# Issuing V of the later batches from GpSimd instead of SyncE in a fused attention and MLP kernel

## The chip, the cores and the metric

The kernel runs on one core of one Trainium2 chip. The metric is the device time of one execution in microseconds. Three runs of the kernel before gave 335.32, 333.19 and 333.25 us, with the median at 333.25 us. One more execution was recorded by the hardware profiler; all views of the profile come from that one.

Engines are called as in the profile: PE is TensorE (its weight loads are PEld), DVE is VectorE, ACT is ScalarE, POOL is GpSimd, SP is SyncE. SP computes nothing here and only issues DMAs; SPq in the profile is its instruction queue.

## The reference

Two stages follow each other. The first is a block-causal attention over 8 batches and 8 heads with 576 positions of 64 elements: a position sees all keys of its own block of 64 and of the blocks before it. The second is an MLP without bias, from 512 to 2048 and back, with a swish of slope beta per hidden unit.

```python
scores = scale * np.matmul(q, k.transpose(0, 1, 3, 2))          # [8, 8, 576, 576]
scores = np.where(block_i >= block_j, scores, -1000000000.0)     # blocks of 64
attn = np.exp(scores - max); attn = attn / (sum(attn) + 1e-09)
x = matmul(attn, v)                                              # -> [4608, 512]
h = x @ w_in                                                     # [4608, 2048]
g = h * (1.0 / (1.0 + np.exp(-beta * h)))
return (g @ w_out).astype(np.float32)                            # [4608, 512]
```

All inputs and the output are float32 in memory; the kernel computes on bf16 and f16 copies.

## The kernel before

**Tiling.** The attention goes in 32 units, four pairs of heads in each of the eight batches b. For a unit, PE multiplies K with Q (L708), ACT takes the exponential (L724), PE multiplies the result with V and with a column of ones for the sum (L764, 30 small matmuls), and DVE divides (L776, L783). The MLP goes in nine chunks of 512 rows. A chunk has 16 groups of four matmuls with w_in (L1000), a tanh on ACT (L1010), a product on DVE (L1014), and then the product with w_out: the plain form for the first chunk (L1036) and a scheme with seven products of half size for the others (L921, with its sums and differences on DVE, L885).

**How Q and K come.** For the first two batches they are loaded in small pieces (L618), cast on POOL (L625) and turned on PE (L634). From b = 2 on (QB is 2), a load brings Q or K of four heads in f32 (L654), POOL casts it to bf16 in two halves (L665), and one DMA transpose turns Q and K of these four heads together (L672); this is called the crossbar's turn here. There are twelve, two per batch. From b = 3 on (XB is 3), the attention's result is turned in the same way by DMA (L800). All these loads and turns are issued by SP, one after the other.

**How V comes.** V of one batch is 1.18 MB in f32. It is loaded by six DMAs: four with 128 positions of all heads (L548, 128 partitions of 8 x 64 elements, 256 KB) and two that bring the last 64 positions, for the even and for the odd heads (L551, 64 KB each). They go into a staging buffer Vs in f32. POOL then casts it, four times two heads, into Vn in bf16 (L574), and L764 reads Vn. The list PARTS says, for each batch, which heads are loaded by whom. In b = 0, four heads of the last pieces are loaded by POOL, cast on the way, straight into Vn; all others are loaded by SP into Vs. Vs has two slots: one of its own and one in the second half of OV. From b = 2 on only the first is used (ts.only), since OV then holds operands of the MLP. So V of a batch may be loaded only after POOL has cast the batch before.

**What sets the order.** A planner (class Plan) lays out all operations at build time. Each operation has an engine, a cost in ns, a priority (lower goes first), dependences and tiles; the planner takes, whenever an engine is free in its own clock, the ready operation of the lowest priority. The order it finds is written out as fixed instruction streams, one per engine, with semaphore waits. On the chip each engine works strictly in that order. For DMAs the planner keeps two queues, H for those that SP and ACT issue and S for those that POOL issues, with a transfer time for each (xfer, 1400 ns for a full piece of V) and a rule for their sharing.

The cost of a V issue is given as 300 + 550 n ns on SP, and 150 + 1450 n ns on POOL, with n = 1 for a full piece and 0.25 for a small one. The loads of SP are also put in one sequence by hand (seq): Q and K of a batch, then its V, each after the one before.

```python
for b in range(B):
    for u in range(4 * b, 4 * b + 4):
        ...
        if u == 4 * b + (3 if b < 2 else 1):
            seq += [o for h0, _, e, _ in PARTS[b] if e == "SP" for o in ld["V", b, h0]]
for x, y in zip(seq, seq[1:]):
    y.after = x
```

POOL's own stream, from about 40 us on, consists of the last weight loads (L507), V's casts (L574) and the casts of Q and K (L665). The weights' DMAs and those few of V in b = 0 are all that POOL's queue (q0) carries; SP's is q1, and the stores of ACT and SP are in the profile's lists of issues under their own lines.

Of the kernel before, what the change touches and what calls it, by code (L numbers as in the profile page):

```python
# [359 lines left out]
def bass_blockwise_causal_attn__then__act_swish_beta_kernel(  # L360
# [10 lines left out]
    with es:  # L371
        def sb(name, shape, dt):
            return es.enter_context(nc.sbuf_tensor(name, shape, dt))
# [1 line left out]
        NQ = 2  # L375
        QB, XB, CAST = 2, 3, "POOL"
        NE = 3
        PARTS = [((0, 4, "SP", range(6)), (4, 8, "SP", range(2)), (4, 8, "POOL", range(2, 6)))] + [((0, 8, "SP", range(6)),)] * 7
        GROUPS = [((0,), (1,), (2,), (3,))] + [((0, 1), (2, 3))] * 7
        NS = 6  # L380
        JOIN = (2,3,4,5,6,7)
# [8 lines left out]
        Vs = [sb("Vs0", [128, 5, 8, 64], f32), OV[:, 2560:5120].rearrange("p (t h d) -> p t h d", t=5, h=8)]  # L390
# [4 lines left out]
        Vn = [sb(f"Vn{i}", [128, 5, 8, 66], bf16) for i in range(NQ)]  # L395
# [25 lines left out]
        P = Plan()  # L421
# [6 lines left out]
        def mm(n):  # L428
            return max(n / 2.4 + 3, 55.0)
# [8 lines left out]
        def pr(u):  # L438
            b, c = divmod(u, NPAIR)
            return u if b < 1 else 10 * u if b < 2 else 994 + 100 * (b - LAG) + 4.9 * c  # L440
# [14 lines left out]
        def mk(fn):  # L455
            return lambda g, e: fn(g)
# [13 lines left out]
        for i in range(NQ):  # L470
# [5 lines left out]
            o = P.op("POOL", 200, mk(lambda g, i=i: g.memset(Vn[i][:, 4, :, 64:66], 0.0)), prio=-5)  # L476
# [6 lines left out]
        for i in range(NQ, NE + 1):  # L483
# [4 lines left out]
                  xfer=100, dma=("d_beta", 1), prio=0.1)  # L488
# [28 lines left out]
        for i in range(NFILL):  # L517
# [10 lines left out]
            n = 125  # L528
            o = P.op("PE", n, ff, deps=[c2, c4], tiles=[tf], lat=n, mode="full", prio=1e6 + i)
# [4 lines left out]
        load, ld, early = {}, {}, []  # L534
        tl = {}
        for b in range(B):
            ts, t = P.tile("Vs"), P.tile("V")
            ts.only = (b,) if b < 2 else (0,)
            early += [ts] * (b < 2)
            tl[b] = t  # L540
            for h0, h1, e, tt in PARTS[b]:

                vs = []
                for i in tt:
                    def fv(g, e, ts=ts, t=t, b=b, h0=h0, h1=h1, i=i):
                        d = Vn[t.slot] if e == "POOL" else Vs[ts.slot]
                        if i < 4:
                            return [g.dma_start(d[:, i, h0:h1, 0:64],  # L548
                                                v[b, h0:h1, 128 * i:128 * i + 128, :].rearrange("h p d -> p h d"))]
                        o = i - 4  # L550
                        return [g.dma_start(d[64 * o:64 * o + 64, 4, h0 + o:h1:2, 0:64],  # L551
                                            v[b, h0 + o:h1:2, 512:576, :].rearrange("h p d -> p h d"))]

                    n = (h1 - h0) / 8 * (1 if i < 4 else 0.25)
                    if e == "SP":
                        o = P.op("SP", 300 + 550 * n, fv, tiles=[ts], xfer=1400 * n,
                                 prio=3.5 + 0.1 * (h0 > 0) if b == 0 else 4 * b + (3.5 if b < 2 else 0.5),
                                 dma=["d_V", h0, 1])
                    else:
                        o = P.op("POOL", 150 + 1450 * n, fv, tiles=[t], xfer=1400 * n, prio=-30 if b == 0 else 4 * b + (3.5 if b < 2 else 0.5), dma=["d_VP", h0, 1])  # L560
                        o.after = lastv if b else None
                    vs.append(o)
                ld["V" if e == "SP" else "VP", b, h0] = vs
                if e == "POOL":
                    lastv = vs[-1]
                    for h in range(h0, h1, 2):
                        load.setdefault(4 * b + h // 2, []).extend([*vs, *ones, *vzero])
                    continue
                n = 5 if 4 in tt else len(tt)
                for g0 in range(h0, h1, 2):  # L570
                    g1 = g0 + 2

                    def fw(g, e, ts=ts, t=t, g0=g0, g1=g1, n=n):
                        return g.tensor_copy(Vn[t.slot][:, 0:n, g0:g1, 0:64], Vs[ts.slot][:, 0:n, g0:g1, :])  # L574

                    o = P.op("POOL", 60 + 60 * n * (g1 - g0), fw, deps=[*vs, *ones, *vzero], tiles=[ts, t],
                             prio=4 * b + 0.5 - (38.5 - 4.6 * (h0 > 0)) * (b < 1))
                    for h in range(g0, g1, 2):
                        load[4 * b + h // 2] = [o]
                lastv = o  # L580
# [12 lines left out]
        def blocks(b):  # L593
            x0 = S * b % RX
            n = min(5, (RX - x0) // 128)
            return [z for z in ((0, n, x0), (n, 5 - n, 0)) if z[1]]
# [4 lines left out]
        for u in range(NU):  # L601
            b, c = divmod(u, NPAIR)
# [7 lines left out]
            if b < QB:  # L610

                turned = []
                for w, (nm, src) in enumerate((("Q", q), ("K", k))):
                    ts, pt = P.tile("ST"), P.tile("P1")
# [6 lines left out]
                    o = ld[nm, u] = P.op("SP", 420, fl, tiles=[ts], xfer=1170, prio=u, dma=["d_S", 0, 1])  # L621
                    o.pkt = 80.0

                    def fn(g, e, ts=ts, tn=tn, p=p, w=w):
# [4 lines left out]
                    o = P.op("POOL" if onp else "DVE", 850 if onp else 750, fn, deps=[o], tiles=[ts, tn],  # L629
                             prio=-40 + 3 * u if onp else -1)  # L630

                    def ft(g, e, tn=tn, pt=pt, p=p, w=w):
                        for i in range(6):
# [4 lines left out]
                    o = P.op("PE", 6 * 43, ft, deps=[o, c4], tiles=[tn, pt, tt_], lat=6 * 43 + 170, mode="full",  # L638
                             prio=pr(u))
# [8 lines left out]
            elif p == 0:  # L648

                for w, (nm, src) in enumerate((("Q", q), ("K", k))):  # L650
                    ts = P.tile("S4")

                    def fl(g, e, ts=ts, src=src, b=b, c=c):
# [3 lines left out]
                    o = P.op("SP", QKI, fl, deps=[o for t in early6 for o in t.users] if b == QB else [],  # L657
                             tiles=[ts], xfer=QKX, prio=u, dma=["d_S4", 0, 1])
# [20 lines left out]
            if b not in JOIN or p == 0:  # L679
# [4 lines left out]
                for grp in visits:  # L684
# [3 lines left out]
                    def fq(g, e, pst=pst, grp=grp, tqk=tqk, b=b):  # L688
                        keep = {}
                        for (uu, g0), ps in zip(grp, pst):  # L690
# [4 lines left out]
                            for t, q0, q1, off in blocks:  # L695
# [17 lines left out]
                    n = sum(220 if g0 < 3 else 60 for _, g0 in grp)  # L713
                    o = P.op("PE", n, fq, deps=cps, tiles=list({id(x): x for x in pst}.values()) + [tqk] + [tes[uu] for uu in sorted({uu for uu, _ in grp})] * (b > 0),
                             lat=n + 200, mode="row", prio=pr(u) + .2 if len(grp) == 4 else pr(u + 1) + .1 if grp[0][0] > u else
                             pr(u) + .1 + .1 * (grp[0][1] >= 2))
# [3 lines left out]
            for g0 in range(4):  # L720
                o, ps = qk[g0]
# [76 lines left out]
            if b >= XB:  # L798
                def fy(g, e, tx=tx, c=c, b=b):
# [4 lines left out]
                n = len(blocks(b))  # L804
                xt.append(P.op("SP", 1300 * n, fy, deps=nrm + (xt[u - 4:u - 3] if b > XB else []), tiles=[tx], xfer=1100,
                               prio=-1, dma=[f"d_TX{n}_", 0, n]))
# [32 lines left out]
        for b in range(B):  # L839
            for u in range(4 * b, 4 * b + 4):  # L840
# [3 lines left out]
# [3 lines that stand above are left out]
# [142 lines left out]
        for r in range(NRC):  # L989
# [5 lines left out]
            for j in range(NJ):  # L995
                ph, tt = P.tile("P1"), P.tile("th")

                def fh(g, e, ph=ph, j=j, row=row):
                    for c in range(4):
# [4 lines left out]
                o = P.op("PE", 4 * mm(512), fh, deps=xd + [win[j // 4]], tiles=[ph, tg], lat=4 * mm(512) + 170,  # L1004
                         mode="full", prio=1000 + 100 * r + j)
# [21 lines left out]
            for w, d0, d1 in [(w, 0, DM) for w in range(4)]:  # L1027
# [4 lines left out]
                o = None  # L1032
                for j0, j1 in parts:
                    def fo(g, e, po=po, tg=tg, w=w, j0=j0, j1=j1, d0=d0, d1=d1):
                        for j in range(j0, j1):
# [4 lines left out]
                    n = (j1 - j0) * mm(d1 - d0)  # L1040
                    was = o
                    o = P.op("PE", n, fo, deps=gs[j0:j1] + wout[j0 // 4:(j1 + 3) // 4],
                             tiles=[po, tg], lat=n + 170, mode="full",
                             prio=1000 + 100 * r + (16 + w + 0.01 * j0 if w == 0 else
                                                     103 + 5.33 * (w - 1) + 1.33 * j0 / 4))
# [84 lines left out]
```

## Time and profile before

| | before |
|---|---|
| median of three runs | 333.25 us |
| profiled execution, device time | 333.59 us |
| its span | 331.8 us |
| instructions | 7478 |
| granted PE clock, mean | 1.0 |
| DMA packets, bytes | 154,993, 53.41 MB |
| of them under 512 B | 139,072 |
| V into Vs from SP, full pieces | 24, median 4.2 us to landing |
| L574 on POOL | 28 casts from Vs, 21.0 us busy, 94.6 us idle ahead of them |
| L665 on POOL | 48 casts, 38.1 us busy, 27.6 us idle ahead |
| L672 from SP | 12 turns, median 7.4 us to landing |
| L800 from SP | 24 turns, median 3.7 us to landing |

The span is the time from the first to the last instruction in the trace; the device time of the same execution is 1.8 us longer. The profiled execution took 0.34 us more than the median of the runs.

A row of a time line gives the start and the length in us, the engine, the line with operation and operands, and the count; brackets at its end give the idle time before it and what ended that. Rows of SPq are issues: their length is the time in which SP was held, not the transfer. A row of windows gives its bounds, its length, then the busy time of PE, PEld, DVE, ACT and POOL, with counts, the PE clock, the share of the DMA engines (the sum over queues, so that it can exceed 1) and GB/s. The table of queues has packets, MB and the share that their packets took of 16 engines' span. In the views of waits, a row has the waiting engine and line, the releaser, the total in us, the number of waits and the longest.

### The profile page before, as it was taken

To read this page: it belongs to the slowest core of one execution; us is meant where nothing else is said; L and a number is where in the kernel's file an instruction comes from. 1 tells how busy PE (TensorE), PEld (TensorE's weight loads), DVE (VectorE), ACT (ScalarE), POOL (GpSimd) and SP (SyncE) were. 2 spreads that over 40 slices of the span, in tenths; PEclk is the share of its full clock that TensorE was granted. 3 is DMA by queue.
4 is the path that set the end of the run, shared out by engine and by line. 5 is a ranking of instruction groups with operands and counts; after the bars stand their busy time and mean duration, and the time that the engine had idled before them with its cause. 6 is when DMAs were issued, how large, how long until landed. Compare 5 with 4: busy or idle time off the path is not lost.

```text
span 331.8 us, 7478 instructions
## 1 busy us (share of the span) xinstructions
PE 321.0 (97%) x3112; PEld 204.1 (62%) x3090; DVE 222.0 (67%) x448; ACT 212.6 (64%) x324; POOL 85.4 (26%) x127
## 2 busy tenths in 40 slices
PE   7898999999999999999999999999999999999996
PEld 4575455545586557754665666576566766666685
DVE  4637775679763898358966595678467685666742
ACT  2876974298457886768757856874875555544521
POOL 6757181056073053103630730240000000000000
PEclk9999999999999999999999999999999999999999
DMA  8999999999999999999999998989102310110023
GB/s 194 227 223 241 207 206 197 210 277 226 189 272 210 210 233 181 201 201 202 179 196 219 221 240 187 158 144 157 35 34 40 87 50 34 55 42 32 2 96 126
DMA packets 154993, 53.41 MB, mean 161 GB/s; under 512 B 139072, under 2 KB 154448, under 8 KB 154960
## 3 DMA queue, kind: packets, MB, share of 16 engines
q1 hardware_dynamic: 141200, 40.19, 64.3%
q0 software_dynamic: 5568, 4.36, 8.4%
q10 hardware_dynamic: 8192, 8.39, 8.1%
q8 instruction: 24, 0.39, 0.5%
q14 instruction: 9, 0.07, 0.1%
HBM read 36.71 MB, written 9.44 MB: 139 GB/s over the span
## 4 chain that ended last, share of the span: by engine, by line
PE 86%; ACT 3%; DVE 2%; SPq 2%; DMA 2%; issue 2%; POOL 1%; POOLq 0%
PE PS L1000 36%; PE PS L921 29%; PE PS L764 8%; PE PS L708 7%; PE PS L1036 4%; DMA Vs<-in_v_dram 2%; ACT E L724 2%; SPq L548 2%; PE PS L813 1%; DVE gT L1014 1%; ACT th L1010 1%; ACT xq L788 1%; DVE xq L783 0%; SPq L551 0%; PE PS L634 0%
## 5 line engine op out<-in xcount | busy, mean ns | idle before, releaser
L1010 ACT ACTIVATE th<-PS,beta 128x512 f32<-128x512 f32 x144 | 96.4, 699 | 59.9 <-PE PS L1000 58.4
L1000 PE MATMUL PS<-xT,w_in 128*128 128x512 bf16 x542 | 130.0, 379 | 2.9 <-issue 0.6
L1014 DVE SCALAR_TENSOR_TENSOR gT<-th,PS 128x512 f16<-128x512 f32 x144 | 95.2, 682 | 30.9 <-ACT th L1010 30.2
L724 ACT ACTIVATE E<-PS 128x1024 bf16<-128x1024 f32 x93 | 92.1, 1028 | 28.4 <-PE PS L708 28.4
L1000 PEld LDWEIGHTS PS<-xT,w_in 128*128 128x128 bf16 x576 | 53.4, 98 | 55.6 <-DVE gT L1014 2.0
L921 PE MATMUL PS<-w_out,gT 128*128 128x256 f16 x512 | 63.0, 273 | 0.0
L921 PEld LDWEIGHTS PS<-w_out,gT 128*128 128x128 f16 x512 | 49.0, 98 | 12.1 <-issue 1.7
L574 POOL CAST Vn<-Vs 128x640 bf16<-128x640 f32 (+1 forms) x28 | 21.0, 751 | 94.6 <-DMA Vs<-in_v_dram 93.2
L665 POOL CAST QKn<-ST 128x640 bf16<-128x640 f32 x48 | 38.1, 794 | 27.6 <-DMA ST<-in_q_dram 13.6
L708 PE MATMUL PS<-QKT 64*128 64x320 bf16 (+4 forms) x328 | 36.4, 297 | 0.2 <-ACT E L724 0.2
L764 PEld LDWEIGHTS PS<-Vn,E 128*128 128x128 bf16 x930 | 30.9, 97 | 4.2 <-POOL Vn L574 0.6
L942 ACT ACTIVATE ost<-PS 128x512 f32<-128x512 f32 x32 | 19.4, 606 | 21.5 <-PE PS L921 21.5
L764 PE MATMUL PS<-Vn,E 128*128 128x65 bf16 x930 | 31.9, 193 | 0.4 <-POOL Vn L574 0.4
L921 PE MATMUL PS<-OV 128*128 128x256 f16 x256 | 32.0, 273 | 0.0
L708 PEld LDWEIGHTS PS<-QKT 64*128 64x128 bf16 (+1 forms) x328 | 13.4, 96 | 25.7 <-issue 11.2
L921 PEld LDWEIGHTS PS<-OV 128*128 128x128 f16 x256 | 24.2, 98 | 5.8 <-issue 0.8
L783 DVE TENSOR_TENSOR xq<-PS,inv 128x640 bf16<-128x640 f32 x30 | 24.7, 822 | 0.8
L885 DVE TENSOR_TENSOR OV<-gT 128x1024 f16<-128x1024 f16 x32 | 24.3, 767 | 1.1 <-PE PS L921 0.6
L730 DVE MEMSET E<- 64x64 uint32 x62 | 6.9, 112 | 23.8 <-ACT E L724 21.8
L945 DVE SCALAR_TENSOR_TENSOR ost<-PS,ost 128x512 f32<-128x512 f32 x22 | 15.1, 688 | 8.3 <-PE PS L921 5.9
L921 PE MATMUL PS<-OV,gT 128*128 128x256 f16 x128 | 16.1, 273 | 0.0
L1036 PE MATMUL PS<-w_out,gT 128*128 128x512 f16 x64 | 15.5, 380 | 0.0
(65 smaller groups left out, 176.1 us busy)
## 6 DMA issues: line engine op xcount, KB each, us to landing
out_dram<-ost ACTq DMA_DIRECT2D x32, 256.0 KB, 4.2
ST<-in_q_dram SPq DMA_DIRECT2D x12, 576.0 KB, 5.7
ST<-in_k_dram SPq DMA_DIRECT2D x12, 576.0 KB, 7.4
Vs<-in_v_dram SPq DMA_DIRECT2D x24, 256.0 KB, 4.2
ST<-in_q_dram SPq DMA_DIRECT2D x8, 288.0 KB, 5.7
ST<-in_k_dram SPq DMA_DIRECT2D x8, 288.0 KB, 6.4
w_in<-in_moe_w_in_dram POOLq DMA_DIRECT2D x4, 512.0 KB, 10.7
w_out<-in_moe_w_out_dram POOLq DMA_DIRECT2D x4, 512.0 KB, 10.1
```

What stands on the lines that cost most here:

```text
L574: return g.tensor_copy(Vn[t.slot][:, 0:n, g0:g1, 0:64], Vs[ts.slot][:, 0:n, g0:g1, :])
L665: return g.tensor_copy(QKn[tn.slot][:].rearrange("p a w n -> p (a w n)")[:, 640 * (2 * a + w):][:, 0:640] .rearrange("p (t h d) -> p t h d ...
L708: z = g.matmul(o, QKT[tqk.slot][r, uu % 2, 1, 128 * t + y:128 * t + m + y], x)
L724: return g.activation(E3[es_(te)][:, g0, :, :], PS[:, ps.slot:ps.slot + 2, :], ACT.Exp, scale=0.125)
L764: z = g.matmul(o, eblk(te, t, i, h), Vn[Tv.slot][:, t, 2 * c + h, 0:65], start=(t == 0), stop=(t == i))
L783: return g.tensor_tensor(xq[xq_(tx)][:].rearrange("p i (h d) -> p h i d", h=2), both(pv, 0, 64), x, ALU.mult)
L885: return P.op("DVE", dve_t(SZ * HC / 2), mk(lambda g: g.tensor_tensor(fo(), fx(), fy(), op)), deps=deps, tiles=tiles, prio=prio)
L921: x = g.matmul(PS[:, pw.slot, HM * w:HM * w + HM], fa()[:, j, 128 * w:128 * w + 128], fb()[:, j, :], start=first and (pair or w == 0) and ...
L1000: z = g.matmul(PS[:, ph.slot, :], w_in[:, c, 128 * j:128 * j + 128], xT[:, c, row % RX:row % RX + RC], start=(c == 0), stop=(c == 3))
L1010: return g.activation(th[tt.slot][:], PS[:, ph.slot, :], ACT.Tanh, scale=beta[:, j:j + 1])
L1014: return g.scalar_tensor_tensor(out=gT[tg.slot][:, j, :], in0=th[tt.slot][:], scalar=1.0, in1=PS[:, ph.slot, :], op0=ALU.add, op1=ALU.mult)
L1036: z = g.matmul(PS[:, po.slot, 0:d1 - d0], gT[tg.slot][:, j, 128 * w:128 * w + 128], w_out[:, j, d0:d1], start=(j == 0), stop=(j == NJ - 1))
```

## The change

From b = 2 on, the six DMAs of V are issued by POOL (a new kind of part, "POOLF") rather than by SP. They bring the same f32 rows to the same staging buffer Vs, and the casts L574 stay. The cost that the planner is told is that of a POOL issue, the priority is 4 b + 0.5, as it was on SP, and a batch's first issue comes after the last cast of the batch before (lastv), the others one after the other. As only parts of SP go into the sequence made by hand, V of these batches leaves it. V of b = 0 and b = 1 is loaded as before. The planner then lays out all five engines anew.

```diff
-        PARTS = [((0, 4, "SP", range(6)), (4, 8, "SP", range(2)), (4, 8, "POOL", range(2, 6)))] + [((0, 8, "SP", range(6)),)] * 7
+        PARTS = [((0, 4, "SP", range(6)), (4, 8, "SP", range(2)), (4, 8, "POOL", range(2, 6)))] + [((0, 8, "POOLF" if b in range(2, 8) else "SP", range(6)),) for b in range(1, 8)]
...
-                        d = Vn[t.slot] if e == "POOL" else Vs[ts.slot]
+                        d = Vn[t.slot] if e == "POOL" and b < 1 else Vs[ts.slot]
...
+                    elif e == "POOLF":
+                        o = P.op("POOL", 150 + 1450 * n, fv, tiles=[ts], xfer=1400 * n, prio=4 * b + 0.5, dma=["d_VF", h0, 1])
+                        o.after = vs[-1] if vs else lastv
                     else:
                         o = P.op("POOL", 150 + 1450 * n, fv, tiles=[t], xfer=1400 * n, prio=-30 if b == 0 else 4 * b + (3.5 if b < 2 else 0.5), dma=["d_VP", h0, 1])
                         o.after = lastv if b else None
                     vs.append(o)
-                ld["V" if e == "SP" else "VP", b, h0] = vs
+                ld["VP" if e == "POOL" else "V", b, h0] = vs
```

## The prediction

> **What bounds the kernel now.** I read the busy shares and the chain of waits first, then the busy time by windows, then the waits by engine, and last the time lines of SP, GpSimd (POOL) and TensorE (PE) around the third and fourth batch (b = 2 and 3).
>
> ```profile
> PE 321.0 (97%) x3112; PEld 204.1 (62%) x3090; DVE 222.0 (67%) x448; ACT 212.6 (64%) x324; POOL 85.4 (26%) x127
> ...
> PE 86%; ACT 3%; DVE 2%; SPq 2%; DMA 2%; issue 2%; POOL 1%; POOLq 0%
> ```
> PE is busy for 321.0 of 331.8 us, and 86% of the chain runs through it. So 10.8 us are idle in all. The windows (length, then PE busy time) say where:
> ```profile
> 0.00:20.00 20.00, 16.77 (x197) 11.04 (x199) 10.27 (x29) 12.10 (x17) 11.65 (x32) 1.00 1.03 199
> 20.00:40.00 20.00, 18.07 (x258) 10.81 (x253) 14.49 (x33) 14.87 (x31) 11.05 (x15) 1.00 1.10 239
> 60.00:80.00 20.00, 19.79 (x109) 8.65 (x105) 15.43 (x28) 14.61 (x22) 8.03 (x10) 1.00 1.17 243
> 220.00:240.00 20.00, 19.74 (x183) 12.47 (x179) 14.40 (x28) 13.84 (x21) 1.44 (x2) 1.00 0.51 91
> ```
> 5.2 us of the gap (3.23 + 1.93) lie ahead of 40 us. From 40 to 320 us the fourteen windows leave 2.8 us together, and some 2.8 us are the end (last eviction and store). The DMA share (last column but one) is above 1.0, queues overlapping, until 220 us and falls to 0.51 then: the transfers are nearly full, but hidden behind PE.
>
> The V transfers are waited for, but by an engine off the path:
> ```profile
> POOL Vn L574 <- DMA Vs<-in_v_dram: 93.2, 7, 18.9
> ```
> No such wait of PE after 40 us is over 0.2 us, except where the trace names none. What counts is the slack between V or Q/K and the PE instruction that needs them:
> ```profile
> 42.76 12.61 SPq L548 DMA_DIRECT2D Vs<-in_v_dram  x3
> 55.41 8.05 SPq L672 DMA_TRANSPOSE QKT<-QKn  x1
> 98.52 3.61 SPq L548 DMA_DIRECT2D Vs<-in_v_dram  x1
> 102.23 3.91 SPq L672 DMA_TRANSPOSE QKT<-QKn  x1
> ```
> ```profile
> 69.03 3.56 POOL L574 CAST Vn<-Vs 128x640 bf16<-128x640 f32 x4 [15.68 <-DMA Vs<-in_v_dram]
> 92.47 3.41 POOL L574 CAST Vn<-Vs 128x640 bf16<-128x640 f32 x4 [10.04 <-DMA Vs<-in_v_dram]
> 95.94 3.48 POOL L665 CAST QKn<-ST 128x640 bf16<-128x640 f32 x4
> ```
> ```profile
> 80.81 1.97 PE L764 MATMUL PS<-Vn,E 128*128 128x65 bf16 x60
> 114.44 0.39 PE L708 MATMUL PS<-QKT 64*128 64x512 bf16 x2
> ```
> For b = 2, V lands at 69.0, its first cast ends near 69.9, and the first L764 that reads it runs at 80.8: 11 us of slack. For b = 3 the cast at 92.5 stands ahead of the Q/K casts at 95.9 on POOL, these ahead of the crossbar's turn at 102.2 on SP; with the median 7.4 us to landing (the page's issue table) it is there at 109.6, and its first L708 runs at 114.4: 4.8 us. Counted the same way, later V casts lead their first L764 by 12 us or more (154.2 against 170.2, and wider).
>
> [...] between 42 and 62 us, with weights on q0, both queues made progress (2112 and 7902 packets). [...] no V issue of the size wanted here is in the trace.
>
> **The change part by part.**
> ```profile
> q1 hardware_dynamic: 141200, 40.19, 64.3%
> q0 software_dynamic: 5568, 4.36, 8.4%
> L548 POOL DMA_DIRECT2D Vn<-in_v_dram x2: 740/745/750, 11.4 to 12.1; - x2
> L551 POOL DMA_DIRECT2D Vn<-in_v_dram x2: 614/616/619, 12.8 to 14.2; - x2
> DMA to landing us min/median/max: 8.0/10.1/14.1
> ```
> *Off SP:* 36 issues, four of 1024 rows of 256 B and two of 256 rows for each of six batches. Their rows after 42 us on SP's time line add up to 46.0 us[...]. None of it is on PE's path, so the credit there is zero. What goes is order: Q/K loads no longer stand behind V, nor V behind SP's wait for an xq (L800).
>
> *On POOL:* 512 rows cost 745 ns and 128 rows 616, or 0.34 ns a row on top of 0.57 us. So 1024 rows are 0.92 us and 256 are 0.66: 4 x 0.92 + 2 x 0.66 = 5.0 us a batch, 30 us in all. Bounds: 4.2 us a batch if the rows were free (as the small ones), 7.4 if the cost went with the rows (4 x 1.49 + 2 x 0.75)[...]. POOL goes from 85 to about 115 of 332 us, so it is no bound. But it works in order: behind V's issues stand the Q/K casts, and behind those the turns, for which L708 waits. A batch takes PE about 30 us, and POOL some 10 of it busy (9.75 of 82 to 112 us): 15 with the issues. Cost on the path, zero, while the slacks above last.
>
> *V's landing.* q1's mean packet is 0.643 x 16 x 331.8 / 141200 = 24.2 ns. V is 4608 rows, 288 an engine: 7.0 us alone, 13.9 us[...]. I take the longer[...]. For b = 2 it is issued behind the four Q/K casts that end at 53.3, but queue 0 still holds w_out, last issued at 47.6 and landing up to 14.1 later, 61.7. So V is there at 69 to 76, the first cast at 77 at the latest, against 81.2 (the comparison of the two instruction orders puts two L1000, 0.4 us, more ahead of it): slack 4 us in place of 11. For b = 3: casts done at 80, issues with two pairs of casts between, first rows 2 us later, landing at 97, V casts to 101, Q/K casts to 104.5, turn there at 112, against 114.4. Slack 2.4 us. With V alone (7 us) all this is 7 us and, for b = 3, 14 us earlier. Later batches have V issued up to a whole batch ahead, with no SP wait before it, and do better than now.
>
> *PE's order.* A planner lays out all engines anew. PE gets the same instructions, the same counts. The first L708 of b = 2 stands 24 L1000 later (24 x 0.216 = 5.2 us), its second visit 11 us; from the fourth unit of b = 2 to that of b = 6 the orders are practically equal; the last L764 stands 4 us earlier, in front of other L1000 and L921. Work is moved among PE's own, so the sum is nil. The added wait is V's semaphore on POOL, as now.
>
> **Sum.** 333.59 us for the profiled execution, minus 0 to 2.8 of gaps, plus 0: I take 333.6 there. The median of the three runs, 333.25, lies 0.3 lower; **333.4 us** is the forecast for the median.
>
> **Rivals.** *V late on queue 0 (slower).* Place: V's cast waits in front of the Q/K casts on POOL in b = 2 and 3. It decides from about 55 ns a packet. At 60 ns V takes 17.3 us: b = 3's V lands near 102, the turn 14.5 later near 117, 2.5 us late; at 72 ns[...] b = 2's first L764 waits 2 us and the turn of b = 3 is there at 123, 8.6 us late in all, and nothing on PE can step in, because its order is fixed. Times 336 to 342. For it: the weights in the same queue and a DMA share above 1.1 there. Against it: with V out of q1, q1 holds only some 290 rows an engine of Q/K and 160 or so for each turn, and is empty part of the time. *SP's relief closes gaps (faster).* Earlier turns let PE's order run without the small waits; at most the 2.8 us between 40 and 320 us: 330.4 to 332.4. Against it: no wait on a turn is among PE's named waits. *POOL as the bound:* 7.4 us a batch[...]; that would delay like the first rival and is counted there. *No real change in V's path:* excluded, the instruction orders show 36 issues on POOL and none left on SP.
>
> **From cases to numbers.** No net effect, 332.4 to 334.6: 0.60. Gaps closed, 330.4 to 332.4: 0.10. V or POOL late, 334.6 to 342: 0.30. About 1%, 3.3 us, is what a measurement tells from no change. Faster by that (under 329.9) needs more than all gaps in mid-run: 0.03. Slower by that (over 336.6) is most of the late case: 0.25. The rest, 0.72, is within. The range, 331.8 to 338.5, takes in the first case, part of the second and the nearer half of the third.
>
> **What will show it.** Right: PE's busy time stays 321 us and its windows between 60 and 120 us stay above 19.5; POOL's V issues read near 0.92 and 0.66 us, busy sum near 115 us; V's landing 7 to 16 us after the last issue; L672 no longer behind L548. Wrong: PE idle with "POOL Vn L574" or a turn's DMA as releaser around 81 or 114 us (first rival), V issues over 1.5 us[...], PE's windows full to 19.95 (second rival). A new gap after 200 us, from L764 or L708 that the planner moved forward, would break the part on PE's order.

## The result, and the profile after

The median after the change is 346.69 us (344.52 to 348.1, four runs), beside 333.48 us for the kernel before on the same chip (333.19 to 335.32, four runs): a ratio of 1.0364 with a 95% interval of 1.0325 to 1.0404. The forecast was 333.4 us, no change. A run more than 1.5% above the fastest of its kernel is called slow, and the ratios in this document are the recorded ones, meant for fast runs, and not the quotients of the medians. The profiled execution took 344.52 us, the least of the four, span 342.6, beside 333.59 and 331.8 before: 10.9 us more, 10.8 in the span.

The changed kernel has three lines more above the loads, so L574, L665, L672, L708, L764, L800 and L1000 are now L577, L668, L675, L711, L767, L803 and L1003. From the page of the kernel after, busy times, granted clock (tenths, 40 slices), queues (packets, MB, share of 16 engines) and the chain:

```profile
PE 327.5 (96%) x3146; PEld 205.5 (60%) x3090; DVE 222.9 (65%) x448; ACT 213.7 (62%) x324; POOL 114.1 (33%) x163
PEclk9998999999996999999999999999999999999999
q1 hardware_dynamic: 112976, 33.11, 55.5%
q0 software_dynamic: 7872, 11.44, 18.2%
PE 61%; DMA 19%; SPq 10%; DVE 4%; POOL 3%; issue 1%; ACT 1%; ACTq 1%; POOLq 0%
```

POOL reads 114.1 us, as forecast, at 33% of the span. But DMA and SP's queue together now hold 29% of the chain, where they held 4%. V is not what is waited for. From the view of POOL's waits before, then from those of POOL and of PE after (total us, count, longest):

```profile
POOL QKn L665 <- DMA ST<-in_k_dram: 11.8, 9, 3.0
```
```profile
POOL QKn L668 <- DMA ST<-in_k_dram: 53.7, 9, 15.2
POOL Vn L577 <- DMA Vs<-in_v_dram: 11.4, 3, 6.0
```
```profile
PE PS L711 <- DMA QKT<-QKn: 4.0, 2, 3.8
PE PS L1003 <- DMA xT<-xq: 2.4, 1, 2.4
```

Before, POOL waited 93.2 us for V and 11.8 us for K. Now it waits 11.4 us for V and 53.7 us for K. The two have changed places, and PE waits for turns (L675 and L803), which are not among its waits before. The time line of PE after shows both waits, and its windows show what follows the first:

```profile
105.44 0.61 PE L711 MATMUL PS<-QKT 64*128 64x512 bf16 x2 [3.83 <-DMA QKT<-QKn]
...
183.47 1.90 PE L1003 MATMUL PS<-xT,w_in 128*128 128x512 bf16 x8 [2.43 <-DMA xT<-xq]
```
```profile
100.00:104.00 4.00, 1.61 (x17) 0.92 (x13) 1.44 (x5) 2.43 (x3) 1.60 (x2) 1.00 1.35 202
104.00:108.00 4.00, 2.56 (x35) 1.90 (x34) 0.11 (x1) 1.48 (x2) 2.58 (x4) 0.51 1.10 197
108.00:112.00 4.00, 4.00 (x32) 2.80 (x29) 1.41 (x4) 1.05 (x2) 2.37 (x4) 0.64 1.42 254
112.00:116.00 4.00, 4.00 (x55) 2.71 (x54) 1.24 (x5) 3.39 (x6) 0.00 (x0) 1.00 1.07 179
```

The third number from the end is the PE clock: 0.51 and 0.64 around and behind the gap (by single us, 0.50 from 105 to 110 us). PE looks full from 108 to 112 us there, but does 32 matmuls where the next window does 55. Slow stretches like this are most of why PE's busy time grew by 6.5 us with equal work: 4.05 us by the bill below. Some 2.4 us more are no work at all: the trace of before lacks 34 records of L1000 (542, and 576 after), and shows small gaps in their place.

The bill, from the start times of the same matmuls in both traces: +1.5 us up to 54 us (a clock of 0.50 from 29 to 32 us, before V of any changed batch; in the runs below it comes and goes in either order: over the first 40 us the clock is 0.96 here and in e15 and 1.00 in e1, and e3, in the changed order, has a mean of 1.0 over its span, so I count it as a difference between executions); +0.6 up to the stall; +2.8 at the stall; +2.55 in the slow stretch behind it (from the first L711 of unit 12 to that of unit 13, 13.24 us in place of 10.69); +2.5 at the second stall (from the first L711 of unit 21 to that of unit 22, 5.75 in place of 3.25; the L1003 between them waits for the xq turn of unit 19); +0.8 after. Sum 10.75.

**How the turn of unit 12 became late.** Unit 12 is the first of b = 3. From the time line of SP before, the load of its K and its turn, and then the time line of SP after:

```profile
66.11 3.04 SPq L654 DMA_DIRECT2D ST<-in_k_dram  x1
...
83.39 4.03 SPq L672 DMA_TRANSPOSE QKT<-QKn  x1
```

```profile
58.47 12.39 SPq L675 DMA_TRANSPOSE QKT<-QKn  x1
70.91 0.57 SPq L657 DMA_DIRECT2D ST<-in_q_dram  x1
72.56 6.69 SPq L675 DMA_TRANSPOSE QKT<-QKn  x1
79.30 0.58 SPq L657 DMA_DIRECT2D ST<-in_k_dram  x1
79.93 4.61 SPq L657 DMA_DIRECT2D ST<-in_q_dram  x1
84.58 5.74 SPq L657 DMA_DIRECT2D ST<-in_k_dram  x1
90.36 4.07 SPq L657 DMA_DIRECT2D ST<-in_q_dram  x1
94.55 5.99 SPq L675 DMA_TRANSPOSE QKT<-QKn  x1
```

The first turn held SP 12.39 us (8.05 before), while V of b = 2 ran on the other queue. K of unit 12 goes out at 79.30, where it went at 66.11 before, and its turn at 94.55 in place of 83.39; it lands at 105.3 (90.3 before), and PE wants it at 101.6. POOL's time line of the same stretch shows V issued and cast in between, with a short wait, and K awaited:

```profile
76.04 1.79 POOL L548 DMA_DIRECT2D Vs<-in_v_dram  x2 [0.30 <-POOL Vn L577]
79.08 1.50 POOL L668 CAST QKn<-ST 128x640 bf16<-128x640 f32 x2 [1.25 <-DMA ST<-in_q_dram]
80.53 1.75 POOL L548 DMA_DIRECT2D Vs<-in_v_dram  x2
82.27 1.25 POOL L551 DMA_DIRECT2D Vs<-in_v_dram  x2
87.43 2.35 POOL L668 CAST QKn<-ST 128x640 bf16<-128x640 f32 x2 [3.91 <-DMA ST<-in_k_dram]
90.61 3.63 POOL L577 CAST Vn<-Vs 128x640 bf16<-128x640 f32 x4 [0.83 <-DMA Vs<-in_v_dram]
```

The queues in the trace of after between 81 and 84 us, with V moving, and then between 84 and 87 us, where few of V's packets move (packets, MB, share):

```profile
q0 software_dynamic: 128, 0.39, 61.5%
q1 hardware_dynamic: 428, 0.10, 24.1%
```
```profile
q1 hardware_dynamic: 1934, 0.49, 106.6%
q0 software_dynamic: 39, 0.16, 23.3%
```

Beside V, queue 1 moves 428 packets in 3 us, and 1934 in the next three, in which few of V's move; the rest of this V follows from 86 to 90 us. The two windows are extremes. A packet of q1 is about 0.23 KB (0.10 MB / 428), near one row of 256 B; one of q0 is 3 KB on the mean. The packets are not one for one (428 against 128), but q0 moves four times q1's bytes (0.39 MB against 0.10). What V's packets are, the totals say. V's 36 issues added 2304 packets to q0 (7872 - 5568) for 27,648 rows. By size, the trace has 1728 packets of 4096 B on q0, and 27,648 / 16 = 1728: 16 rows of 256 B in each. The other 576 have 4 B: 16 for each of 36 issues. The trace of before could not show this: its 5568 packets are weights (eight DMAs of 528) and V of b = 0 (1280 rows + 64), cast on the way, at one row a packet.

### The profile page after: what moved, and what is told of

Same layout as the page of the kernel before. It is cut to its first block, busy times and chain, and to the rows that moved or that the text cites. A ratio compares the mean times of both kernels' runs of the same rounds, so it can differ in the third digit from the quotient of the medians.

```text
span 342.6 us, 7520 instructions
## 1 busy us (share of the span) xinstructions
PE 327.5 (96%) x3146; PEld 205.5 (60%) x3090; DVE 222.9 (65%) x448; ACT 213.7 (62%) x324; POOL 114.1 (33%) x163
## 3 DMA queue, kind: packets, MB, share of 16 engines
q0 software_dynamic: 7872, 11.44, 18.2%
q10 hardware_dynamic: 8192, 8.39, 7.7%
## 4 chain that ended last, share of the span: by engine, by line
PE 61%; DMA 19%; SPq 10%; DVE 4%; POOL 3%; issue 1%; ACT 1%; ACTq 1%; POOLq 0%
PE PS L1003 27%; PE PS L924 24%; DMA ST<-in_k_dram 11%; PE PS L767 5%; PE PS L711 5%; SPq L548 5%; SPq L657 3%; DMA QKT<-QKn 3%; DMA xT<-xq 2%; DMA Vs<-in_v_dram 2%; DVE gT L1017 2%; POOL Vn L577 2%; DVE OV L888 1%; SPq L675 1%; SPq L551 1%
## 5 line engine op out<-in xcount | busy, mean ns | idle before, releaser
L1003 PE MATMUL PS<-xT,w_in 128*128 128x512 bf16 x576 | 137.5, 381 | 2.6 <-DMA xT<-xq 2.4
L1003 PEld LDWEIGHTS PS<-xT,w_in 128*128 128x128 bf16 x576 | 53.6, 98 | 58.8 <-DMA xT<-xq 2.7
L924 PE MATMUL PS<-w_out,gT 128*128 128x256 f16 x512 | 64.6, 277 | 0.5 <-DVE gT L1017 0.5
L668 POOL CAST QKn<-ST 128x640 bf16<-128x640 f32 x48 | 39.4, 821 | 66.9 <-DMA ST<-in_k_dram 53.7
L711 PE MATMUL PS<-QKT 64*64 64x64 bf16 (+4 forms) x328 | 37.3, 302 | 4.1 <-DMA QKT<-QKn 4.0
L767 PEld LDWEIGHTS PS<-Vn,E 128*128 128x128 bf16 x930 | 31.6, 98 | 5.1 <-POOL Vn L577 0.9
L767 PE MATMUL PS<-Vn,E 128*128 128x65 bf16 x930 | 32.8, 195 | 0.7 <-POOL Vn L577 0.7
L711 PEld LDWEIGHTS PS<-QKT 64*128 64x128 bf16 (+1 forms) x328 | 13.6, 96 | 29.6 <-issue 15.4
L577 POOL CAST Vn<-Vs 128x640 bf16<-128x640 f32 (+1 forms) x28 | 20.1, 718 | 18.7 <-DMA Vs<-in_v_dram 11.4
L548 POOL DMA_DIRECT2D Vs<-in_v_dram x24 | 21.3, 893 | 8.0 <-issue 6.7
```

The costliest lines, as they stand in the source:

```text
L548: return [g.dma_start(d[:, i, h0:h1, 0:64], v[b, h0:h1, 128 * i:128 * i + 128, :].rearrange("h p d -> p h d"))]
L668: return g.tensor_copy(QKn[tn.slot][:].rearrange("p a w n -> p (a w n)")[:, 640 * (2 * a + w):][:, 0:640] .rearrange("p (t h d) -> p t h d ...
L711: z = g.matmul(o, QKT[tqk.slot][r, uu % 2, 1, 128 * t + y:128 * t + m + y], x)
L767: z = g.matmul(o, eblk(te, t, i, h), Vn[Tv.slot][:, t, 2 * c + h, 0:65], start=(t == 0), stop=(t == i))
L924: x = g.matmul(PS[:, pw.slot, HM * w:HM * w + HM], fa()[:, j, 128 * w:128 * w + 128], fb()[:, j, :], start=first and (pair or w == 0) and ...
L1003: z = g.matmul(PS[:, ph.slot, :], w_in[:, c, 128 * j:128 * j + 128], xT[:, c, row % RX:row % RX + RC], start=(c == 0), stop=(c == 3))
```

## The experiments

Before the first run there were three theories for the 3.6%: **packets** (V on q0, in packets of 16 rows, holds back what q1 moves), **POOL** (its 29 us of issuing stand ahead of the Q/K casts), and **the order** (the planner's new layout is worse by itself). The table has the median, the range, and the recorded ratio to the kernel before on the same chip, whose medians were 335.02 us (e1 to e4), 334.69 (e5 to e8), 334.43 (e9 to e12) and 334.58 (e13 to e15).

| | order of | V from | median us (range) | ratio (95%) |
|---|---|---|---|---|
| the change | after | POOL | 346.69 (344.52–348.1) | 1.0364 (1.0325–1.0404) |
| e1 | before | POOL | 346.98 (341.59–348.74) | 1.0384 (1.0313–1.0455) |
| e2 | after | SP | 344.91 (344.24–346.35) | 1.0311 (1.0259–1.0363) |
| e3 | after | POOL, 1/8 of the heads | 335.89 (334.54–338.48) | 1.0048 (1.0025–1.0072) |
| e11 | after | POOL, 1/2 of the heads | 335.69 (334.64–338.17) | 1.0056 (1.0036–1.0076) |
| e12 | before | SP, 1/8 | 335.66 (333.3–337.75) | 1.0013 (0.9989–1.0037) |
| e13 | before | POOL, 1/8 | 334.55 (333.13–336.36) | 1.0001 (0.9978–1.0025) |
| e14 | before | POOL, one-row packets | 334.08 (332.63–336.74) | 0.9993 (0.997–1.0016) |
| e15 | before | ACT | 335.68 (333.19–339.12) | 1.0028 (1.0–1.0056) |
| e5 | after | POOL, one-row packets | 342.4 (340.14–349.39) | 1.0184 (1.01–1.0267) |
| e8 | after | ACT | 341.84 (338.45–342.37) | 1.0168 (1.0088–1.0248) |
| e4 | anew | POOL, cast into Vn | 353.89 (349.56–355.94) | 1.053 (1.0435–1.0626) |
| e7 | anew | POOL | 357.26 (351.28–358.79) | none on record |
| e6 | after | POOL, PE kept busy | 347.15 (346.1–351.97) | 1.0339 (1.0236–1.0441) |
| e10 | after | POOL, held once | 348.74 (347.65–350.02) | 1.0427 (1.039–1.0465) |
| e9 | after | POOL, held twice | 344.54 (340.85–353.77) | 1.0278 (1.0244–1.0313) |

### The queue and the order exchanged: e1 and e2

e1 keeps the order of the kernel before on every engine and hands the 36 issues to POOL once the plan is made, at the places where SP had them. (Parts of a load carry their batch as isv.)

```diff
...
         P.schedule()
+        moved = [o for o in P.order["SP"] if getattr(o, "isv", 0) >= 2]
+        for o in moved:
+            o.eng, o.dma = "POOL", ["d_VF", 0, 1]
+        P.order["SP"] = [o for o in P.order["SP"] if o not in moved]
+        P.order["POOL"] = sorted(P.order["POOL"] + moved, key=lambda o: o.start)
```


> The layout of the kernel before on PE, ACT, DVE, with only the 36 V issues of the third batch on moved, after planning, from SP's stream to POOL's at their planned places. Packet theory (on queue 0 V goes in packets of 16 rows, since 7.08 MB came in 2304 packets, and takes the DMA engines nearly alone for some 6 us a batch, while Q/K loads and turns on queue 1 go row by row and stand still): slower than before, 337 to 346 us, with turns above 9 us to landing. Layout theory (the planner's new order alone is slow, wherever V comes from): 333 to 335 us. POOL theory (29 us of V issues on POOL hold back the casts behind them): 337 to 346 us.

e2 is the reverse: the order of the changed kernel, with the 36 issues handed to SP by the same lines, SP and POOL exchanged.

> The layout of the changed kernel, with only the 36 V issues moved, after planning, back from POOL's stream to SP's at their planned places. Packet theory: most of the loss goes, 333 to 337 us, turns back near 7.4 us to landing. Layout theory: it stays, 343 to 348 us. POOL theory: it goes, 333 to 337 us.

Both lose, so either is enough by itself. e1's four runs lie 2.0, 3.2, 3.9 and 4.1% above 335.02 us, so I read its 1.0384 as a loss of 2 to 4%. e1 is the cleaner, since all engines but POOL and SP run the sequence of the kernel before, and V starts at nearly the old times (the first issue of b = 3 at 73.1 us against 75.4, of b = 6 at 161.3 against 161.5; the last of a batch goes out up to 11.5 us earlier; a full piece held POOL for some 0.89 us and SP, before, for up to 4.8). Still two turns come late. From PE's time line in e1:

```profile
178.20 0.39 PE L709 MATMUL PS<-QKT 64*128 64x512 bf16 x2 [2.40 <-DMA QKT<-QKn]
209.28 2.62 PE L1001 MATMUL PS<-xT,w_in 128*128 128x512 bf16 x7 [2.63 <-DMA xT<-xq]
```

From one unit's first L709 to the next, against before: 5.72 us in place of 3.24 at the first stall, 7.54 in place of 5.88 behind it, 13.77 in place of 9.56 around the second. That is 8.35 us; the two profiled executions differ by 8.00 (341.59 and 333.59). The QKT turn that is late is that of unit 22, the one with the least slack in the kernel before: it landed there at 174.7, 1.5 us before PE wanted it. In e2, which has no V of the later batches on q0, the QKT turns land in 6.1 us at the median, as its packet theory had it, but PE also waits for turns, 2.5 us for QKT and 5.5 us for xT. There V stands in SP's own sequence at the places that the planner had chosen for POOL, and the turns and loads stand behind it, which I take for the reason; no run tests it alone.

### Less of V: e3, e11 and e12

These load only some heads of V from b = 2 on, by the same 36 issues; the casts and matmuls read what was in Vs (a memset at 31 us fills what nothing else writes).

```diff
+                        if b > 1:
+                            h1 = h0 + (1 if i < 4 else i - 3)     # e3, e12;  e11: h1 = h0 + 4
...
```


> The changed kernel with the same 36 issues on POOL in the same places, but each brings one head of eight only (the other heads' V is left out, so the result is not the reference's; one memset of 0.9 us is added on DVE near 31 us). Packet theory: with 1/8 of the rows on queue 0 the stalls near 105 and 183 us go, 332 to 336 us. POOL theory: POOL's issues take 0.6 us each instead of 0.9, so two thirds of the hold-up stay, 340 to 345 us. Layout theory: 338 to 346 us, since the order stays, though it has less to move.

> The changed kernel with the same 36 issues on POOL, bringing four heads of eight (the other four heads' V of the later batches is left out, so the result is not the reference's; one memset of 0.9 us is added on DVE). If the loss is in the rows that queue 0 moves, it lies between the 335.9 us of one head and the 346.7 us of eight, near 338 to 342 us. If the loss came with the issues or the layout, 344 us or more.

> The kernel before, V from SP in its own layout, with one head of eight in each V issue of the later batches (the others left out, so the result is not the reference's; one memset of 0.9 us is added on DVE). The kernel before hides V behind PE, so taking V's rows away gives nothing: 332 to 335 us, within 1% of the kernel before. If V's transfer costs something already there: under 331 us.

e3 has the changed order and 105.2 us of POOL, and is within 0.5% of the kernel before, as only its packet theory had it; e11, with half of V's rows, is within 0.6%. No wait for a turn is left in either trace; what is left in both is 1.06 us ahead of the first L714 of unit 12, for ACT's exponential. So the new order and the number of POOL's issues cost about half a per cent when V is small. e11 was expected in the middle; the loss isn't proportional to the rows, but sets in somewhere between half of them and all, though half of them still come mostly in packets of 16 (768 of 4096 B, 192 of 2048 B). e12 says that V's transfer on SP costs the kernel before nothing: there was nothing to win.

### The packets: e5 and e8, then e13 to e15

e5 lets V's DMA cast to bf16, into half of Vs, which makes q0's packets single rows (33,792 packets in place of 7872); POOL then copies bf16.

```diff
+        Vb = Vs[0][:].bitcast(bf16)
...
-                        d = Vn[t.slot] if e == "POOL" and b < 1 else Vs[ts.slot]
+                        d = Vn[t.slot] if e == "POOL" and b < 1 else Vs[ts.slot] if b < 2 else Vb
...
```


> The changed kernel in its own layout, with V of the third batch on cast to bf16 on the way into the first half of each staged row, so that queue 0 has one row in a packet and not sixteen; same 36 issues, same POOL casts (bf16 to bf16). Arbitration theory[...]: queue 1 keeps about half its rows while V moves, against a fifth now, the turns come back to 7 to 8.5 us to landing, the stalls near 105 and 183 us shrink, 334 to 340 us. Volume theory (the DMA engines are full, so V, wherever it moves beside Q/K and the turns, takes their time and only the plan's order decides): turns stay near 10 us and the time at 343 to 349 us.

e8 hands the 36 issues to ACT, by the lines of e1 with POOL and ACT in the roles of SP and POOL. ACT's queue moved V's f32 rows one by one (q10 has 36,416 packets = 8192 + 27,648 + 576).

> The layout of the changed kernel, with the 36 V issues moved after planning from POOL's stream to ACT's at their planned places, so that V goes by a third queue, row by row, and POOL only casts. Arbitration theory: the turns come back to 7 to 8.5 us to landing; the ACT stream holds some 0.6 us for each issue, 22 us in all beside 214 busy; 334 to 342 us. Volume theory: 343 us or more, turns near 10 us.

Both take back about half of the loss (1.0184 and 1.0168 in place of 1.0364), and neither takes back all: the intervals of both, 1.01 to 1.0267 and 1.0088 to 1.0248, lie above 1 and below that of the change. In e8 no turn stalls PE; its largest wait is 2.95 us for gT at 68 us, and ACT had been held by V's issues until 66.5 us, so part of its rest is ACT's. The QKT turns' median landing stayed near 10 us in both (10.2, in an execution of 349.39 us, the longest of e5, and 9.7), so the expectation of 7 to 8.5 us fell for both. This left open whether the other half was the order, or any second queue. The last three kernels ask it in the order of the kernel before: e13 is e1 with one head, e14 is e1 with e5's edit, e15 is e1 with ACT in place of POOL.

> The order of the kernel before on all engines, V from batch 2 on issued by POOL at SP's planned places as in e1 (346.98 us), but one head of eight: the same 36 issues, an eighth of the rows. The other heads of V are not loaded, so the output is wrong for them. If the rows on queue 0 are what slows queue 1: 334 to 337 us, QKT landing 5 to 6 us. If POOL's 28 us of issuing in front of the Q/K casts are: 344 us or more.

> As e1, but V is cast to bf16 by its DMA into half of Vs, so that queue 0 moves one row a packet instead of 16; the casts on POOL then copy bf16. V is issued at about the times of the kernel before (e1 had them within 10 us). If the size of queue 0's packets is the whole cause: 334 to 337 us, QKT landing under 8.5 us. If any second queue beside queue 1 costs, and the packets only a part, as e5 had it in the other layout: 339 to 343 us, QKT 9 to 10.5. If the packets play no part: 346 us or more.

> As e1, but ACT issues V (row by row, on the queue of the stores), at SP's planned places. POOL issues nothing more. If POOL's issuing were the cause: 334 to 336 us plus what ACT's issuing costs ACT. If a second queue beside queue 1 costs, with single rows less than with packets of 16: 338 to 342 us as e8, with QKT landing near 9.7 us. 346 us or more would mean that the kind of queue plays no part.

All three are within 0.3% of the kernel before, and e14 differs from e1 in V's packets and in the type of what they deliver. V's issues go out within 5 us of e1's, and POOL issues as long (29.3 us in all, 29.0 in e1). In e13 the turns land in 7.3 us at the median, not in 5 to 6. The queues' totals of e1, then of e14:

```profile
q1 hardware_dynamic: 112976, 33.11, 56.8%
q0 software_dynamic: 7872, 11.44, 18.7%
```
```profile
q1 hardware_dynamic: 112976, 33.11, 56.6%
q0 software_dynamic: 33792, 7.90, 26.3%
```

33,792 = 5568 + 27,648 + 576: one row a packet, and a larger share of the DMA engines than in e1 (26.3% against 18.7%). It costs nothing measurable all the same. From e14, between 82 and 86 us, with V moving:

```profile
q0 software_dynamic: 1638, 0.21, 82.4%
q1 hardware_dynamic: 1469, 0.37, 69.4%
```

Over these 4 us the two move about as many packets, though not evenly: in the first of them q0 has 1030 and q1 104. Such windows only illustrate (e1 has 1261 packets of q1 from 82 to 86 us, with less V in that stretch). Counted over all half-microseconds from 57 to 215 us in which at least three of q0's packets start, q1 starts 214 packets a us in the changed kernel, 259 in e1 and 345 in e14, and 700 to 745 in the others in which SP has a load or turn under way. So q1 does lose less beside single rows; how the engines choose between the queues is not shown by it.

That less is written (bf16) is not the reason in e15: it moves all of V in f32, row by row, at 1.0028, though on ACT's queue. On POOL's queue all of V's f32 rows came only in packets of 16 (1728 of 4096 B), so there the two weren't told apart. In the order of the kernel before, then, the form in which q0 carries V accounts for the whole loss of e1, within the intervals, and POOL's issuing, the second queue and the lost place in SP's sequence are none of it. In the changed order e5 has single rows on q0 too, and q1 its 350 packets a us beside them, and 1.8% stays: by the medians, about half of the change's loss is not in the packets. One reading of mine was too simple: the median landing of QKT in e14 is 10.2 us (11.5 in e1, 7.4 in e15), and yet PE waits for no turn there; its one long wait, 1.76 us, is for ACT. A median over twelve turns does not say whether the one turn with little slack is late.

### One stall repaired: e6, e10 and e9

e6 puts 30 matmuls that nobody reads in front of the stalled L711, so that PE does not idle there. e10 makes V of b = 4 wait for the turn of unit 12; e9 also makes V of b = 7 wait for the xq turn of unit 19.

```diff
+        z = P.op("PE", 3300, fk, deps=[d for d in hold[0].deps if d.engs != ("SP",)])   # e6
...
+        for bb, w in ((4, 12),):                          # e10;  e9: ((4, 12), (7, (19,)))
+            w = turns[w] if isinstance(w, int) else xt[w[0]]
...
+                o.deps.append(w)
```


> The changed kernel with 30 idle matmuls of 256 columns (3.3 us at full clock) on PE right ahead of the first L711 of the fourth batch, where it idles 3.8 us for a turn; they wait only for their bank. If the halved clock after that gap is due to the idle time, the stretch from this L711 to the next pair's first one takes 10.7 us as in the kernel before, and not 13.2, and the total falls by 2 to 3 us to about 344. If the clock falls for another reason, the stretch stays at 13.2 us.

> As the kernel with both held, but only V of the fifth batch waits. Collision theory: the stall at 105 us and the clock after it go (the stretch to the next pair's L711 is 10.7 us), but the L1003 at 183 us waits for its turn until the same time as before, so most comes back there: 344 to 347 us. Otherwise: 346 to 348 us, with the stall at 105 us still there.

> The changed kernel, same layout on PE, ACT, DVE and SP; on POOL only two sets of V issues wait: those of the fifth batch for the landing of the turn that the first L711 of the fourth batch needs (the 3.8 us stall at 105 us), those of the last batch for the landing of the xq turn that the L1003 at 183 us needs, behind two more pairs of casts. Collision theory (V's rows on queue 0 take the DMA engines from just these two turns): both stalls shrink to under 1 us and the halved clock goes, 346.7 - 2.8 - 2.5 - 2.5, so 338 to 341 us. If V's rows are not what delays these turns, 344 to 348 us.

e6 bears out what was expected of the clock: the stretch behind unit 12 takes 10.69 us again, and not 13.24. Yet the total is as before the repair (347.15 us, 344 expected), because the next late turn takes it back. PE's wait for the xq turn of unit 19 in e6, then in e10:

```profile
185.00 3.22 PE L1005 MATMUL PS<-xT,w_in 128*128 128x512 bf16 x8 [6.20 <-DMA xT<-xq]
```
```profile
185.88 3.60 PE L1006 MATMUL PS<-xT,w_in 128*128 128x512 bf16 x8 [9.10 <-DMA xT<-xq]
```

PE arrives earlier and waits longer (2.43 us in the change, 6.20 and 9.10 here): the second turn does not come sooner, since PE starts at 185.00 and 185.88 in place of 183.47. e10 also shows that V of b = 4 was not the immediate cause at unit 12: its turn went out at 91.7, with none of that V under way, took 11.9 us to land (10.8 in the change), and PE still waited 1.69 us. By the time line of SP above the lateness comes from further up, from b = 2 and 3; no run shows that alone. e9, at 1.0278, takes back about a quarter of the loss and misses its 338 to 341 us. Its profiled execution was its slowest of seven, 353.77 us, so it doesn't speak for the others: there the stall for the xq turn of unit 19 is gone, that at unit 12 stays (2.49 us), and new ones stand at 149 us (1.79 us for a V cast) and 161 us (6.93 us for an xq turn). In that execution, holding V back moved the lateness on.

### Planned anew: e4 and e7

e4 uses the path that the kernel before has for parts of b = 0: V cast on the way, straight into Vn, no POOL casts. e7 tells the planner a smaller cost for the issue and large packets on q0 (P.PKT).

```diff
+        PARTS = [...] + [((0, 8, "POOL" if b > 1 else "SP", range(6)),) for b in range(1, 8)]     # e4
...
+                        o = P.op("POOL", 590 + 330 * n, fv, tiles=[ts], ...)     # e7
+                        o.pkt = P.PKT
```


> V of the third batch on is issued by POOL as bf16, cast on the way straight into Vn, without staging and without the POOL casts of V; the planner lays out anew. The weights, cast in the same way, have one row in a packet (528 packets for 512 rows and 16 ends). Packet theory: [...] queue 0 shows about 288 packets an engine and batch; turns near 7 to 9 us, 333 to 338 us. POOL theory: issues cost as much, casts are saved: 336 to 342 us. Layout theory: open, as the order is another.

> The changed kernel with the planner told what the trace shows: V's issue on POOL costs 590 + 330 n ns, and while V moves, queue 1 gets a fifth of its rate (V is given the packet weight of the MLP's weights). All engines are laid out anew. If a plan that rested on the wrong share was the cause, 333 to 338 us, and the first L708 of the fourth batch waits for no turn. If full DMA engines leave no room for V at POOL's times whatever the plan, 340 us or more.

Both are the slowest of all. Their profiled executions, of 355.94 and 357.68 us, have QKT stalls of 6.3 and 5.8 us near 81 us, and again waits for xq's turns. e4 has one-row packets (q0: 33,792), so a new layout can lose 5% without large packets. Why these layouts are worse was not followed up.

No kernel beat the one before.

## Why the prediction failed

**The bound and its cover** were read rightly: PE bound, V waited for by POOL alone, no gain to be had. e12 and e13 confirm the last. One reading was off: of the 2.8 us that PE's windows leave from 40 to 320 us, some 2.4 are the records that the trace lacks; e12, with the same order on PE and all 576 of L1000, leaves 0.46. So "SP's relief closes gaps" had even less to win than it said.

**POOL's price** held. V's issues after, from the answer by tile (durations in ns min/median/max, first and last start):

```profile
L548 POOL DMA_DIRECT2D Vs<-in_v_dram x24: 882/890/907, 57.5 to 176.7; - x24
L551 POOL DMA_DIRECT2D Vs<-in_v_dram x12: 621/637/667, 61.0 to 179.7; - x12
```

Forecast were 0.92 and 0.66 us. With DVE 65% busy, the longest of each is 25 and 46 ns above the shortest. That this time costs nothing on the path in the order of the kernel before is shown by e14 (29.3 us of issues, 0.9993).

**"V's landing" is the step that failed.** Its 13.9 us were an estimate of mine: 288 rows an engine at 24.2 ns, 7.0 us, doubled because q1 moves beside V. No trace showed the doubling. It charged the sharing of the engines to V alone, and left q1 as it was: the turn still "there" 7.4 us after its issue, at no cost. Of V it was right or too careful. V of b = 2 was complete at 70.6 us (forecast 69 to 76), that of b = 3 at 90.6 (forecast 97), and each batch 7.1 to 12.1 us after its last issue (forecast 7 to 16). The slow party was q1. Its turns took 9.9 us (7.4 before) and xq's 4.4 (3.7), its Q loads 8.4 (5.7) by the pages' medians, and the turn of unit 12 landed 15 us later than before. e1 against e14 isolates V's form on q0 in the order of the kernel before: +2 to 4% against none.

The step also went by rows, from q1's mean packet of 24.2 ns, and did not ask how many rows a packet of each queue has: 16 in V's on q0 (1728 packets of 4096 B), one in q1's (106,752 packets of 256 B). Nor did the two queues move packet for packet: q1 had 3.3 packets for one of q0 in the window of the changed kernel (428 against 128).

**"q1 ... is empty part of the time"**, the argument against the first rival, named the wrong victim. It asked whether q1 would hold up V; what mattered was the time in which q1 was not empty and moved less beside V (428 packets in 3 us, then 1934 in the next three). Its count was of half a batch, too: a batch has four Q/K loads of 144 rows an engine and two turns of 160, 896 rows, which at its own 24.2 ns fill, by that estimate, 21.7 of PE's 30 us a batch, without xq's turns. Little was empty. Of the Q/K loads the text costed nothing. The xq turns (L800), whose lateness made the second stall, appear only as something V used to stand behind.

**The turn that was watched** was the second of b = 3 (102.2 us, first L708 at 114.4, slack 4.8 us). The one that failed is the first: issued at 83.39 before, there at 90.3, wanted at 100.3. It had 10 us of slack and lost all of them. In e1 it was that of unit 22, which had 1.5 us and which the prediction passed over with "Later batches ... do better than now". Counting the slack behind one turn was not enough where all loads and turns share a sequence.

**PE's order, "the sum is nil"**, is the second step that failed. It nearly holds for small V (e3, 1.0048), but the order was costed by itself. With full V, the changed order keeps 1.8% even without large packets (e5; 1.7% in e8, some of it ACT's), and e2 loses 3.1% with V on SP. In the order of the kernel before the same forms of V leave nothing (e14, e15). So the new order is less tolerant of V's rows; which part of it (V's earlier places, or Q/K's later ones) was not told apart.

**The first rival** had the direction and nearly the place, and came nearest in size, though 346.69 lies beyond its 336 to 342. Its carrier was wrong: it had V late in front of the Q/K casts, and V came early. Its sums are loose as well: carried through both batches from its own 97 and 112, 60 ns a packet put the turn of b = 3 near 119 and 72 ns near 126, where it has 117 and 123. No term was there for the clock behind a gap, 2.55 us.

**The new issuer** was charged only with the time of its issues. e1 changes the issuer, and with it the queue and the form of V's packets (2304 on q0 for 27,648 rows), and costs 2 to 4%.

## What to carry to other kernels

Here, V on another engine's queue also changed how fast q1 moved beside it (259 packets a us in e1, 345 in e14): take packets and MB of each queue from the profile, in the same stretch, and ask who is slowed, not only whether the moved transfer arrives. An uncast load on POOL's queue beside a row-by-row queue that feeds the critical path was the bad case here (2 to 4% in e1); the same load in one-row packets, or from ACT's queue, cost nothing measurable in the order of the kernel before (0.9993 and 1.0028), and some 1.7 to 1.8% in the changed one. In a fixed instruction order, follow every stream with a deadline to the end, and list the slack of each arrival: repairing the first late one only lengthened the wait for the next (2.43 us in the change, 6.20 in e6).

## What the runs showed of the hardware

- q0 took V's f32 rows of 256 B in packets of 16 (after: 1728 of 4096 B and 576 of 4 B), and in e14, where it cast them, one by one: 28,224 packets for the same 27,648 rows, 576 beyond them again. q1 moved V, and Q and K from b = 2 on, in single rows (134,400 packets of 256 B before and 106,752 after, 27,648 fewer), and so did ACT's q10 with V (e15: 36,416 = 8192 + 27,648 + 576).
- The fewer, larger packets let V land in about the same time (6.5 us in e1, 7.0 in e14, medians of the 256 KB pieces), but the kernel loses 2 to 4% with them and nothing without; the single-row form occupies more of the DMA engines (26.3% against 18.7%).
- A wait of 3.83 us in the changed kernel came with a PE clock of 0.50 from 105 to 110 us; in e6, with matmuls in that gap, the stretch behind it took 10.69 us in place of 13.24. In the changed kernel the 2.43 us wait at 183 us left the clock at 1.00 (183 to 195 us), and in e10 the stretch behind a wait of 1.69 us at 103.7 us took 10.69 us, too. But in e1 gaps of 2.40 and 2.63 us were followed by a clock of 0.68 (180 to 184 us; 1.66 us lost in the unit behind the gap) and 0.61 (209 to 213 us), and in e14 seven L1003 behind a gap of 1.76 us took 3.18 us, where seven at 170 us took 1.67. The length of one gap does not decide it alone in these runs.
